# Fourth unit in the Strassen stays, joined attention groups two pairs behind, shared keys, three raw weight buffers, first loads on ScalarE's queue, halved last block

## The chip, the cores and the metric

The kernel runs on one core of a Trainium2 chip. The metric is the device time of one launch in microseconds (us); the times are medians over several runs. TensorE (PE) multiplies matrices, VectorE (DVE) and ScalarE (ACT) do the elementwise work, GpSimd (POOL) does small things, and SyncE (SP) issues the DMAs.

## The reference

Attention over 4 batches, 8 heads, 768 positions, 64 values per head, in which a query sees the 96 keys up to its own and the first 8 keys of its sequence, with a slope on the distance; behind it a gated feed-forward layer in float32:

```
keep = is_global | is_local          # first 8 keys, or 0 <= rel < 96
bias = -slopes[:, None, None] * dist[None, :, :]
scores = scores + bias[None, :, :, :]
...
a = np.exp(scores)
a = a / (np.sum(a, axis=-1, keepdims=True) + 1e-09)
x = (a @ v) as 3072 tokens x 512
out = ((x @ w_a) * (x @ w_b)) @ w_out    # w_a, w_b: 512 x 1536, w_out: 1536 x 512
```

## The kernel before

**Units and weights.** The 3072 tokens are six units of 512 tokens (`NU`, `T`). The 1536 columns of the layer are six pieces of 256, called fp 0 to 5. Weights arrive as float64 words and are turned into float32 on ACT and DVE (`to32`, the tiles `wr` for raw words and `wm` for the result). Each number is then split into a high and a low part, and a product is three matmuls (high by high, high by low, low by high).

**Passes.** `STAYS` says which pieces lie in SBUF together and which units pass over them. In the first stay (fp 0, 1, 2; units 0, 1, 2, 3) products are plain: `project_plain`, L1022, four groups of 12 matmuls 512 wide for each unit and piece. In the five later stays they are Strassen products: `project`, L1001, seven groups of 12 matmuls 256 wide, with sums on DVE (L1110) and sums of the inputs (`forms`, the tiles `xT` and `xf`). Behind either come 24 matmuls 512 wide into four accumulators (`back`, L1178). Units 0 to 3 do their remaining pieces in the stays (3, 4) and (5), units 4 and 5 do all of theirs in the later stays. Weight forms for later stays are written to DRAM (`dw`) and loaded again (`wl`).

**Attention.** A granule is one pair of heads of one unit: 24 score matmuls (`ps`, L709), the masked subtraction on DVE (L677), the exponential on ACT (L693), the sum plus 1e-9 and its reciprocal on DVE (L772, L779), the scaling on DVE or ACT (L792, L789), a transposition, and the product with the values (`pa`, L341). Unit 0 transposes on PE (L826, L827); the others transpose on DVE (L808) and go through DRAM (`mir`) into the tiles `px` and `py`. Units 1 to 3 (`LAGGED`) do the scores in two halves and the values one granule later, all as blocks of their own. Units 4 and 5 (`JOINED`) emit the scores of one granule and the values of the one before it as one block, in which matmuls on different quarters of the array stand next to each other (L709 and L322). The attention outputs of units 0 to 3 (`NEAR`) stay in the tile `X` when they are made; those of 4 and 5 go to DRAM (`dx`) and are loaded into `X` when their pass comes.

**What sets the order.** All work goes into a planner (`Schedule`): every operation has a due time, costs per engine and the buffers it takes, and the planner lists the engines' instructions in the order in which its own model would start them. The constants at the file's head (`SPANS` for attention, `CONV` for conversions, `QUADS0` and others) are due times, in passes or in nanoseconds. The engines then run in that order, each waiting only for what it needs. DMAs all go out from SP in the planned order.

**Start and end.** Before the planned part, SP loads the two counts, the position table, the slopes and the keys and queries of two granules; DVE computes the counts and a flag (L1520 to L1531) on which all engines branch. Then DVE makes the distances from the table (L604 to L608) and eight mask halves (L615). At the end `close` adds the accumulators to an earlier partial result (L1239) and writes four blocks of 128 x 512.

Of the kernel before, what the change touches and what calls it, by code (L numbers as in the profile page):

```python
# [25 lines left out]
P = 128  # L26
# [10 lines left out]
KB = KW + 64  # L37
# [8 lines left out]
KN = NH * KB  # L46
# [3 lines left out]
    ((0, 1, 2), (0, 1, 2, 3), True),  # L50
    ((3, 4), (3, 2, 1, 0), False),
    ((5,), (0, 1, 2, 3), False),
    ((5, 2), (4, 5), False),
    ((3, 4), (5, 4), False),
    ((0, 1), (4, 5), False),
)
PASSES = [(k, u) for k, stay in enumerate(STAYS) for u in stay[1]]
SPANS = {1: (0.0, 0.6), 2: (0.85, 1.6), 3: (1.6, 2.6), 4: (3, 7), 5: (6.79, 11.5)}
NEAR = (0, 1, 2, 3)
CONV = {3: (1.72, 2.88), 4: (2.5, 3.5), 5: (4.39, 7), 2: (7.27, 10), 0: (10, 12.27), 1: (11.39, 14)}  # L60
# [9 lines left out]
    "psT": (("acc3", "ga"), ("acc3",)),  # L70
}
LATER = {"psS": ("psS", "psA"), "psA": "psA", "psT": "psS"}
LAGGED = (1, 2, 3)
JOINED = (4, 5)
JOINT = 2920.0
# [6 lines left out]
WSBUFS = 2  # L82
# [3 lines left out]
FORM0 = 2410.0  # L86
START = 25980.0
LOADLEAD = 7790.0
VLAG = 13280.0
# [3 lines left out]
LAGS = {"pe": 200.0, "act": 270.0, "dve": 230.0, "pool": 290.0, "dma": 2300.0}  # L93
BIG = float(2**38)
HALF0 = 24080.0
HALF1 = 35730.0
STEPS0 = (-9.53, 6000.0, 17000.0, 25000.0)
QUADS0 = (4000.0, 3150.0, 9670.0, 13270.0, 22000.0, 25000.0)
QUADS1 = (28400.0, 31000.0, 36000.0, 35540.0, 46130.0, 44380.0)
QUADS2 = (48000.0, 51000.0, 54000.0, 51210.0, 58890.0, 63000.0)  # L100
GAP = 20220.0


def entry(u, g, i):
# [188 lines left out]
class Values:  # L293
# [91 lines left out]
    def __call__(self):  # L385
        self.main.plan.op(self.due, self.emit, self.reads, self.claim(), pe=1900)
        self.take(self.due)


class Fast:  # L390
    def __init__(self, ctx, tc, a, out, nf, ident, tiles=()):
        self.tc, self.nc = tc, tc.nc
        self.a, self.out, self.nf, self.ident = a, out, nf, ident
        self.ctx = ctx
        self.tiles = dict(tiles)
        self.plan = Schedule()
        self.count = 0
        self.granule = 0
        self.turns = 0
        self.late = None  # L400
# [51 lines left out]
    def to32(self, fp, piece, due, tag):  # L452
        nc, op = self.nc, self.plan.op
        n = f"{fp}_{piece}"
        raw = self.sbuf([P, 2 * CN], I32, "wraw", "wr" + n, 2)
# [7 lines left out]
            due - 6000.0,  # L463
# [115 lines left out]
    def load_w(self, fp, due, step):  # L579
        for j, name in enumerate(FORMS + ("O0", "O1")):  # L580
# [4 lines left out]
            self.dma(at - 5000.0, lambda st=st: st[:, :], lambda d=d: d[:, :], [d], [st], CN * 4 * P)  # L585
# [6 lines left out]
    def masks(self):  # L592
        nc, op = self.nc, self.plan.op
        ng, nl = self.nf[:, 0:1], self.nf[:, 1:2]
# [4 lines left out]
        part = lambda i: full[:, :].rearrange("p a b -> p (a b)")[:, i * n : i * n + n]  # L599
        rel, key, tmp = (lambda: part(0)), (lambda: part(1)), (lambda: part(2))  # L600

        def steps(e):
            v = nc.vector
            v.tensor_scalar(tmp(), rel(), nl, BIG, op0=ALU.is_ge, op1=ALU.mult)  # L604
            v.tensor_scalar(key(), key(), ng, BIG, op0=ALU.is_ge, op1=ALU.mult)
            v.tensor_add(rel(), rel(), tmp())
            v.tensor_scalar(key(), key(), nl, None, op0=ALU.add)
            v.tensor_tensor(rel(), rel(), key(), op=ALU.min)  # L608

        op(-2e5, steps, [], [full], port=BOTH, dve=3 * dve(n, True) + 2 * dve(n))  # L610
        for hd in range(H):
            p, h = divmod(hd, 2)
            op(
                -1e5 + hd if p < 2 else 4000.0 + hd,
                lambda e, p=p, h=h, hd=hd: nc.vector.tensor_scalar(  # L615
                    self.mask[p][:, h].rearrange("p a b -> p (a b)"),
                    rel(),
                    self.slope[:, hd : hd + 1],
                    None,
                    op0=ALU.mult,  # L620
                ),
# [3 lines left out]
                dve=dve(n, True),  # L625
# [22 lines left out]
    def granule_ops(self, u, p, due, x, d, before):  # L648
# [57 lines left out]
        def score(i, h, bank, c0, s, c, k, w):  # L706
            rows = slice(64 * h, 64 * h + 64)
            q0, k0 = i * P, QN + i * KB
# [11 lines left out]
        if u in JOINED:  # L720
# [3 lines left out]
            ahead = before  # L724
# [21 lines left out]
            before = None  # L746
        for r in () if u in JOINED else range(2):
# [10 lines left out]
            op(due, scores, [qk], ps, pe=720)  # L758
# [6 lines left out]
        if u not in DIRECT:  # L765
            tt = self.sbuf([P, 6, 2 * NH * 32], F32, "tt", "tt" + n, TTBUFS)
        for half in range(2):
            js = range(4 * half, 4 * half + 4)
            jw = slice(4 * half, 4 * half + 4)
            op(  # L770
                due,
                lambda e, jw=jw: nc.vector.tensor_scalar_add(sm[:, 2, jw], sm[:, 1, jw], 1e-9),  # L772
                [(sm, j) for j in js],
                [(sm, ("d", half))],
                dve=70,
            )
            op(
                due,
                lambda e, jw=jw: nc.vector.reciprocal(sm[:, 3, jw], sm[:, 2, jw]),  # L779
                [(sm, ("d", half))],  # L780
                [(sm, ("r", half))],
                dve=80,
            )
            flat = lambda: t[:, :].rearrange("p a b c -> p (a b) c")

            def norm(e, js=js, jw=jw):
# [3 lines left out]
                else:  # L790
                    for j in js:
                        nc.vector.tensor_scalar(  # L792
                            flat()[:, j], flat()[:, j], sm[:, 3, j : j + 1], None, op0=ALU.mult
                        )

            ts = [(t, j) for j in js]
            op(due, norm, [(sm, ("r", half))], ts, port=BOTH, dve=4 * dve(KW, True), act=4 * (act(KW) + 100))

            if u in DIRECT:
                for i in range(2 * half, 2 * half + 2):  # L800
                    self.direct(u, p, n, i, due, t, px, py)
# [11 lines left out]
            op(due, turn, ts, [(tt, half)], dve=dve(512) + dve(256))  # L813
        if u not in DIRECT:
            self.carry(n, due, tt, px, py)

        return Values(self, u, p, vt, px, py, x, d, due + VLAG)

    def direct(self, u, p, n, i, due, t, px, py):
        nc = self.nc  # L820
        self.turns += 1
        bank = self.bank(self.early_bank("psT", u, p, self.turns), f"pt{n}_{i}")

        def turn(e):
            for h in range(2):
                nc.tensor.transpose(bank[:104, h * P : h * P + P], t[:, i, h, :KX], self.ident)  # L826
                nc.tensor.transpose(  # L827
                    bank[:64, 256 + h * P : 256 + h * P + P], t[:, i, h, KX:], self.ident
                )

        self.plan.op(due, turn, [(t, 2 * i), (t, 2 * i + 1)], [bank], pe=4 * 109 + 60)
        self.copy(
            due,
            lambda: px[:104, :, 2 * i : 2 * i + 2].rearrange("p g j k -> p j g k"),
            lambda: bank[:104, :256].rearrange("p (j g k) -> p j g k", j=2, g=4),
            256,
            [bank],
            [(px, ("b", i))],
            psum=True,
        )  # L840
        for s in range(2):
            self.copy(
                due,
                lambda s=s: py[64 * s : 64 * s + 64, 2 * s : 2 * s + 2, 2 * i : 2 * i + 2].rearrange(
# [836 lines left out]
```

## Time and profile before

| What | before |
|---|---|
| median of 3 runs | 722.39 us (721.56 to 723.73) |
| time of the profiled execution | 722.86 us |
| its span from first to last instruction | 721.0 us |
| mean granted TensorE clock | 0.990 |
| ACT busy | 384.9 us (53%) |
| DMA moved | 162.43 MB, mean 225 GB/s |

The span leaves out 1.9 us of the profiled time that lie around it. Times inside the trace count from the start of the span. PE, the busiest engine, is read stretch by stretch further down. Busy time of PE is modelled: matmuls overlap, so a row's duration is longer than the distance to the next matmul, and costs of PE work are taken from distances between starts.

### The profile page before, as it was taken

Reading aid. Unit: us, or ns where it says so; the run is one execution under the profiler, and the core shown is the slowest. Engines: PE = TensorE matmul, PEld = TensorE weight load, DVE = VectorE, ACT = ScalarE, POOL = GpSimd, SP = SyncE. Lnnn points to the kernel's source line nnn. Section 1 sums busy time; section 2 is a strip of 40 time slices with the busy share of each in tenths; the row PEclk is TensorE's granted clock in tenths of the full one; section 3 lists DMA queues with packets and bytes.
Section 4 is the critical chain, followed back from the end, with each engine's and each line's share of the span. In section 5 each row is a group of like instructions: output and inputs, shape, how many; then the busy total and the mean of one; then the engine's idle time right before and its main releaser. Section 6 shows DMA issues by size and latency. Waiting matters only on the chain.

```text
span 721.0 us, 15565 instructions
## 1 busy us (share of the span) xinstructions
PE 685.9 (95%) x5808; PEld 602.3 (84%) x5808; DVE 581.6 (81%) x1552; ACT 384.9 (53%) x988; POOL 1.8 (0%) x8
## 2 busy tenths in 40 slices
PE   5598999999999999999999999999999999999995
PEld 4487877777777888888999998999898999999994
DVE  7999897878697776899899997999988558646652
ACT  5988675845565674566554546566434434424220
POOL 1000000000000000000000000000000000000000
PEclk9889999999999999999999999999999999999998
DMA  8547888998989997776786888748893423533121
GB/s 299 190 165 284 252 270 294 314 287 285 293 295 293 264 322 250 255 243 213 260 295 234 302 262 282 261 161 275 292 293 142 132 81 97 160 117 103 59 75 63
DMA packets 67910, 162.43 MB, mean 225 GB/s; under 512 B 8433, under 2 KB 21873, under 8 KB 66033
## 3 DMA queue, kind: packets, MB, share of 16 engines
q1 hardware_dynamic: 67824, 161.34, 67.7%
q8 instruction: 48, 0.79, 0.4%
q14 instruction: 38, 0.30, 0.1%
HBM read 110.45 MB, written 50.86 MB: 224 GB/s over the span
## 4 chain that ended last, share of the span: by engine, by line
PE 70%; DVE 13%; DMA 10%; ACT 4%; issue 2%; SPq 0%; ACTq 0%; DVEq 0%
PE acc L1178 22%; PE al L1001 16%; PE ga L1001 12%; PE ps L709 4%; DMA wr<-wts 3%; PE pa L341 3%; DMA qk<-qk 2%; DMA wl_A<-dw_A 1%; DVE t L677 1%; DVE tt L808 1%; DMA X<-dx 1%; DVE t L792 1%; DVE wm L495 1%; PE ps_al L322 1%; ACT wm L470 1%
## 5 line engine op out<-in xcount | busy, mean ns | idle before, releaser
L1178 PE MATMUL acc<-w_O,hh 128*128 128x512 f32 x576 | 197.0, 400 | 0.0
L1178 PEld LDWEIGHTS acc<-w_O,hh 128*128 128x128 f32 x576 | 108.3, 188 | 24.9 <-issue 1.5
L1178 PE MATMUL acc<-w_O,hl 128*128 128x512 f32 x288 | 113.7, 395 | 0.8 <-DVE hl L443 0.8
L693 ACT ACTIVATE t<-t,sm 128x168 f32<-128x168 f32 x192 | 81.1, 425 | 15.7 <-DVE sm L677 15.6
L1001 PE MATMUL al<-xf_T,w_S 128*128 128x256 f32 x576 | 76.7, 283 | 0.7 <-ACT s L433 0.7
L1001 PEld LDWEIGHTS al<-xf_T,w_S 128*128 128x128 f32 x576 | 72.4, 189 | 1.4 <-ACT s L433 0.9
L1178 PEld LDWEIGHTS acc<-w_O,hl 128*128 128x128 f32 x288 | 54.3, 188 | 10.8 <-DVE hl L443 1.4
L433 ACT CAST hh<-h 128x512 fp32r<-128x512 f32 (+1 forms) x61 | 36.0, 592 | 48.2 <-DVE h L443 23.6
L470 ACT ACTIVATE wm<-wr 128x512 f32<-128x512 f32 x54 | 36.2, 671 | 42.6 <-DMA wr<-wts 25.5
L709 PEld LDWEIGHTS ps<-qk 64*64 64x64 f32 x1056 | 32.8, 141 | 26.7 <-issue 14.0
L433 ACT COPY s<-al 128x512 f32<-128x512 f32 x44 | 25.7, 584 | 54.0 <-PE al L1001 53.8
L443 DVE TENSOR_TENSOR hl<-h,hh 128x512 fp32r<-128x512 f32 (+1 forms) x78 | 49.8, 644 | 4.9 <-ACT hh L433 4.5
L709 PE MATMUL ps<-qk 64*64 64x104 f32 (+2 forms) x1056 | 39.3, 276 | 14.5 <-DMA qk<-qk 7.1
L677 DVE CUSTOM_DVE_ANT_0 t<-ps,mask 128x168 f32<-128x168 f32 x176 | 48.6, 326 | 3.2 <-PE ps L709 3.0
L1110 DVE TENSOR_TENSOR s<-ga,s 128x512 f32<-128x512 f32 x48 | 32.8, 684 | 15.2 <-PE ga L1001 15.0
L808 DVE STREAM_TRANSPOSE tt<-t 128x512 f32<-128x512 f32 x80 | 40.9, 553 | 1.2 <-DMA mir<-tt 0.6
L1001 PE MATMUL ga<-xf_T,w_S 128*128 128x256 f32 x288 | 38.5, 283 | 1.1 <-DVE s L1110 1.0
L1001 PEld LDWEIGHTS al<-xf_B,w_A 128*128 128x128 f32 x288 | 37.5, 188 | 2.2
L505 ACT ACTIVATE wr<-wr 128x512 int32<-128x512 uint32 x54 | 36.1, 672 | 4.8 <-DVE xf_B L443 2.6
L1001 PE MATMUL ga<-xf_B,w_A 128*128 128x256 f32 x288 | 38.3, 283 | 0.3 <-DVE s L1110 0.3
L1001 PEld LDWEIGHTS ga<-xf_T,w_S 128*128 128x128 f32 x288 | 36.4, 188 | 2.6 <-DVE s L1110 2.0
L1001 PE MATMUL al<-xf_T,w_A 128*128 128x256 f32 x288 | 38.5, 283 | 0.1
(292 smaller groups left out, 1351.5 us busy)
## 6 DMA issues: line engine op xcount, KB each, us to landing
wr<-wts SPq DMA_DIRECT2D x54, 512.0 KB
qk<-qk SPq DMA_DIRECT2D x24, 720.0 KB
mir<-tt SPq DMA_DIRECT2D x20, 768.0 KB
vt<-vd SPq DMA_DIRECT2D x24, 512.0 KB
X<-dx SPq DMA_DIRECT2D x10, 1024.0 KB
part<-o SPq DMA_DIRECT2D x32, 256.0 KB
wl_S<-dw_S SPq DMA_DIRECT2D x32, 256.0 KB
px<-mir SPq DMA_DIRECT2D x60, 128.0 KB
```

The lines of the kernel that those rows point to most:

```text
L341: self.main.nc.tensor.matmul(self.banks[0][64 * h : 64 * h + 64, o : o + P], self.vt[:lanes, v0 : v0 + 64], src[:, :, 2 * i + h], start=c ...
L433: self.nc.scalar.copy(out(), src())
L443: lambda e: self.nc.vector.tensor_tensor(out(), a(), b(), op=op),
L470: lambda e: nc.scalar.activation(m(), high().bitcast(F32), AF.Abs),
L505: lambda e: nc.scalar.activation(low(), low().bitcast(U32), AF.Copy, scale=2.0**-29),
L677: lambda e: nc.vector.tensor_tensor_reduce(t[:, i, h], bank[:, c0 : c0 + KW], self.mask[pair][:, h, kind], -0.125, 3.0e38, ALU.add, ALU.mi ...
L693: lambda e: nc.scalar.activation(t[:, i, h], t[:, i, h], AF.Exp, bias=sm[:, 0, j : j + 1], scale=-1.0, accum_out=sm[:, 1, j : j + 1],),
L709: nc.tensor.matmul(bank[64 * s : 64 * s + 64, c0 + c : c0 + c + w], qk[rows, q0 + 64 * s : q0 + 64 * s + 64], qk[rows, k0 + k : k0 + k + w ...
L808: nc.vector.transpose(dst[:, :, e0 : e0 + n], src[:, :, c0 : c0 + 32 * n].rearrange("p j (e k) -> p j e k", e=n),)
L1001: self.nc.tensor.matmul(bank[:, ab * HT : ab * HT + HT], w[:, a, (2 * ab + c) * P : (2 * ab + c) * P + P], x[:, b, c], start=first, stop=F ...
L1110: lambda e: nc.vector.tensor_tensor(s[:, :], bank[:, :], s[:, :], op=ALU.add),
L1178: self.nc.tensor.matmul(acc[i][:, :], a[:, rows], w[:, b], start=first and f == 0 and k == 0, stop=False, skip_group_check=True,)
```

## The change

1. `STAYS` loses its lists of units; `TURNS` holds them. Unit 3 leaves the first stay. It passes over fp 3 and 4 behind unit 1, opens the stay (5, 2) with units 4 and 5 after it, and ends the kernel over fp 0 and 1. The number of passes stays 18.
2. Unit 3 joins `JOINED` and leaves `NEAR` and `LAGGED`. The values in a joined block are those of the granule two before (`BEHIND`), and granules wait in one list through units 3, 4 and 5.
3. The keys of neighbouring blocks are stored once: 1152 columns for a granule in place of 1440 (unit 0: 1248, in an array of its own).
4. Raw weight words get three buffers in place of two, and weight forms that are loaded again three in place of two.
5. The first keys and queries are loaded in two halves from ACT's queue. The distances are made ahead of the branch with two ACT and two DVE operations in place of five DVE operations, and mask halves may go to ACT.
6. The sum plus 1e-9 goes to POOL, once for eight columns outside unit 0. Where DVE scales, it does four columns in one operation. Unit 0's first two granules copy two transposed blocks at a time out of PSUM.
7. The last accumulator is computed, added and written in two halves.
8. All due times are new.

```diff
-    ((0, 1, 2), (0, 1, 2, 3), True),
...
+    ((0, 1, 2), True),
...
+TURNS = ((0, 1, 2), (2, 1, 3, 0), (0, 1, 2), (3, 4, 5), (5, 4), (4, 5, 3))
-NEAR = (0, 1, 2, 3)
+NEAR = (0, 1, 2)
-LAGGED = (1, 2, 3)
-JOINED = (4, 5)
+LAGGED = (1, 2)
+JOINED = (3, 4, 5)
+BEHIND = 2
-WSBUFS = 2
+WSBUFS = 3
+WRBUFS = 3
...
-        raw = self.sbuf([P, 2 * CN], I32, "wraw", "wr" + n, 2)
+        raw = self.sbuf([P, 2 * CN], I32, "wraw", "wr" + n, WRBUFS)
...
-            ahead = before
+            ahead = self.waiting.pop(0)[0] if len(self.waiting) == BEHIND else None
...
+                for _, carry in self.waiting[:1]:
+                    carry()
...
+        def sums(jw, js, k):
+            op(
+                due,
+                lambda e: nc.gpsimd.tensor_scalar_add(sm[:, 2, jw], sm[:, 1, jw], 1e-9),
...
-                    for j in js:
-                        nc.vector.tensor_scalar(
-                            flat()[:, j], flat()[:, j], sm[:, 3, j : j + 1], None, op0=ALU.mult
-                        )
+                    nc.vector.tensor_tensor(
+                        flat()[:, jw],
+                        flat()[:, jw],
+                        sm[:, 3, jw].unsqueeze(2).to_broadcast([P, 4, KW]),
+                        op=ALU.mult,
+                    )
...
+                cuts = ((0, 256), (256, 512)) if split and f == 1 and i == 3 else ((0, 512),)
...
         nc.sync.dma_start(nv, a["ns"].to_broadcast([P, 2]))
+        nc.scalar.dma_start(tiles["qk0"][:, :RUN], a["qf"][0, :, :RUN])
+        nc.sync.dma_start(table[:, :width], a["pos"][:, :width])
+        nc.scalar.dma_start(tiles["qk0"][:, RUN:], a["qf"][0, :, RUN:])
+        nc.sync.dma_start(tiles["slope"], a["pos"][:, width:])
+        nc.sync.dma_start(tiles["qk1"], a["qf"][1])
...
+def build_distances(nc, few, far, table):
+    n = 2 * KW
+    rel, key, tmp = (table[:, i * n : i * n + n] for i in range(3))
+    nc.scalar.activation(tmp, rel, AF.Relu, bias=far[:, 1:2], scale=BIG)
+    nc.scalar.activation(key, key, AF.Relu, bias=far[:, 0:1], scale=BIG)
+    nc.vector.tensor_add(rel, rel, tmp)
+    nc.vector.scalar_tensor_tensor(rel, key, few[:, 1:2], rel, op0=ALU.add, op1=ALU.min)
```

On DVE at the start, from the branch on all flags to the first masked subtraction, there stood in the kernel before:

```order
L1558 COMPARE_AND_BRANCH
L604 TENSOR_SCALAR X<-X,nf 128x336
L605 TENSOR_SCALAR X<-X,nf 128x336
L606 TENSOR_TENSOR X<-X 128x336
L607 TENSOR_SCALAR X<-X,nf 128x336
L608 TENSOR_TENSOR X<-X 128x336
L615 TENSOR_SCALAR mask_154<-X,slope 128x336 x2
L615 TENSOR_SCALAR mask_157<-X,slope 128x336 x2
L677 ISA t_0_160,sm_0_161<-ps_0_0_0_114,mask_154 128x168
```

In the changed kernel the same place of DVE's queue, with the two distance operations ahead of the branch, is:

```order
L1639 TENSOR_TENSOR X<-X 128x336
L1640 SCALAR_TENSOR_TENSOR X<-X,counts 128x336
L1621 TENSOR_LOAD flag
L1624 COMPARE_AND_BRANCH
L622 TENSOR_SCALAR mask_132<-X,slope 128x336
L622 TENSOR_SCALAR mask_139<-X,slope 128x336
L622 TENSOR_SCALAR mask_143<-X,slope 128x336
L622 TENSOR_SCALAR mask_160<-X,slope 128x336
L684 ISA t_0_162,sm_0_163<-ps_0_0_0_118,mask_132 128x168
```

Five operations on the table became two, and four mask halves (one of each pair of heads) are left; the other four stand in ACT's queue.

On PE, in the kernel before, the values of unit 3's first granule (`pa`; `px` and `py` are the transposed weights of attention, `vt` the values) stand as a block of their own between two plain groups of unit 2's pass, and the scores of unit 3's third granule follow as another block:

```order
L1022 MATMUL al_1_1(0, 1)_2742<-xp_3_2454,w_A_0_924 128x512 x3
L341 MATMUL pa_0_2767<-px_248,vt_0_2406 64x128 x2
L341 MATMUL pa_0_2767<-py_133,vt_0_2406 64x128 x2
...
L1022 MATMUL ga_1_1(0, 1)_2794<-xp_0_2333,w_A_0_852 128x512 x3
...
L709 MATMUL ps_2_0_0_2814<-qk_78 64x168
L709 MATMUL ps_2_0_1_2816<-qk_78 64x168
```

In the changed kernel the values of unit 3 stand in shared blocks. This one, in the second stay, ends the scores of unit 4's first granule (`ps_0`), goes on with the values of unit 3's third granule (`vt_2`, the one two before), and is followed by accumulation:

```order
L716 MATMUL ps_0_al<-qk_59 64x64
L716 MATMUL ps_0_ga<-qk_59 64x64
L336 MATMUL ps_0_al<-py_135,vt_2_2967 64x64 x2
L336 MATMUL ps_0_ga<-py_135,vt_2_2967 64x64 x2
...
L336 MATMUL ps_0_al<-px_246,vt_2_2967 64x64 x2
L336 MATMUL ps_0_ga<-px_246,vt_2_2967 64x64 x2
...
L1226 MATMUL acc_3_2772<-w_O_192359_2936,hh_3_1_3262 128x512
```

Unit 3's values moved out of blocks of their own into blocks shared with scores, and from the first stay's end into the second stay; there are ten shared blocks in place of seven.

More of the change, by code (lines that the diff above doesn't have):

```diff
@@ L36 @@
 KW = KX + 64
-KB = KW + 64
+KB = NG + P
 T = 512
@@ L399, in __init__ @@
         self.turns = 0
-        self.late = None
+        self.waiting = []
     def open(self):
@@ L766, in granule_ops @@
             tt = self.sbuf([P, 6, 2 * NH * 32], F32, "tt", "tt" + n, TTBUFS)
+        whole = u not in DIRECT
+        def sums(jw, js, k):
+            op(
+                due,
+                lambda e: nc.gpsimd.tensor_scalar_add(sm[:, 2, jw], sm[:, 1, jw], 1e-9),
+                [(sm, j) for j in js],
+                [(sm, ("d", k))],
+                pool=170,
+            )
+            op(
+                due,
+                lambda e: nc.vector.reciprocal(sm[:, 3, jw], sm[:, 2, jw]),
+                [(sm, ("d", k))],
+                [(sm, ("r", k))],
+                dve=100,
+            )
+        if whole:
+            sums(slice(0, 2 * NH), range(2 * NH), 0)
         for half in range(2):
@@ L769, in granule_ops @@
             jw = slice(4 * half, 4 * half + 4)
[L770 to L775, printed above, removed]
-            )
[L777 to L783, printed above, removed]
+            if not whole:
+                sums(jw, js, half)
             flat = lambda: t[:, :].rearrange("p a b c -> p (a b) c")
@@ L820, in direct @@
+        return then
+    def direct(self, u, p, n, blocks, due, t, px, py):
         nc = self.nc
         self.turns += 1
-        bank = self.bank(self.early_bank("psT", u, p, self.turns), f"pt{n}_{i}")
+        i0, m = blocks[0], 2 * len(blocks)
+        js = slice(2 * i0, 2 * i0 + m)
+        bx = self.bank(self.early_bank("psT", u, p, self.turns), f"pt{n}_{i0}")
+        by, c0 = (bx, 2 * P) if m == 2 else (self.bank("ga", f"pu{n}_{i0}"), 0)
         def turn(e):
[L825 to L829, printed above, removed]
@@ L831, in direct @@
-        self.plan.op(due, turn, [(t, 2 * i), (t, 2 * i + 1)], [bank], pe=4 * 109 + 60)
+            for k in range(m):
+                i, h = i0 + k // 2, k % 2
+                o = k * P
+                nc.tensor.transpose(bx[:104, o : o + P], t[:, i, h, :KX], self.ident)
+                nc.tensor.transpose(by[:64, c0 + o : c0 + o + P], t[:, i, h, KX:], self.ident)
+        self.plan.op(
+            due,
+            turn,
+            [(t, j) for j in range(js.start, js.stop)],
+            [bx] if m == 2 else [bx, by],
+            pe=m * 2 * 109 + 60,
+        )
@@ L832, in direct @@
         self.copy(
             due,
[L834 to L838, printed above, removed]
+            lambda: px[:104, :, js].rearrange("p g j k -> p j g k"),
+            lambda: bx[:104, : m * P].rearrange("p (j g k) -> p j g k", g=4, k=32),
+            m * P,
+            [bx],
+            [(px, ("b", i)) for i in blocks],
@@ L892, in attention @@
             self.xsaved[u] = d
-        late, self.late = self.late, None
+        late = None
         for p in range(NPAIR):
             then = self.granule_ops(u, p, dues[p], x, d, late)
-            if u in LAGGED or u in JOINED:
+            if u in LAGGED:
                 late = then
-            else:
+            elif u not in JOINED:
                 then()
-        if late and u in JOINED and u + 1 in JOINED:
-            self.late = late
-        elif late:
+        if late:
             late()
+        if u == JOINED[-1]:
+            for k, (then, carry) in enumerate(self.waiting):
+                if k:
+                    carry()
+                then()
         return x
@@ L1162, in project, with back @@
         return parts
-    def back(self, fp, due, parts, acc, first):
+    def back(self, fp, due, parts, acc, first, split):
         st = 3 * pe(512)
@@ L1280, in run @@
             t = times[i]
-            fps, _, plain = STAYS[stay]
+            fps, plain = STAYS[stay]
             if i and PASSES[i - 1][1] != u:
@@ L1287, in run @@
                     xf[u] = self.load_x(u, t - 7000.0)
-            elif i and STAYS[PASSES[i - 1][0]][2] and not plain:
+            elif i and STAYS[PASSES[i - 1][0]][1] and not plain:
                 xf[u] = self.forms(u, t - 7000.0, x)
@@ L1316, in prev @@
                 def prev(d, fp=fp, parts=parts, acc=acc, first=fresh and k == 0, over=over, u=u, i=i):
-                    self.back(fp, d, parts, acc, first)
+                    self.back(fp, d, parts, acc, first, over and i + 1 == len(PASSES))
                     d = d[-1] if isinstance(d, list) else d
```

283 lines of the change are left out of this document (155 added, 128 removed).

## The prediction

> **What bounds the kernel now.** I read the busy shares first, then busy time by stretches, then who PE waits for, and then single places in the timeline and the chain of waits. On the page:
>
> ```profile
> PE 685.9 (95%) x5808; PEld 602.3 (84%) x5808; DVE 581.6 (81%) x1552; ACT 384.9 (53%) x988; POOL 1.8 (0%) x8
> ```
>
> PE is the bound as a mean. The stretches show where it is not (columns: busy time of PE, weight loads, DVE, ACT and POOL with their instructions, granted clock, DMA share, GB/s):
>
> ```profile
> core 0: us, PE busy (x) PEld busy (x) DVE busy (x) ACT busy (x) POOL busy (x), PEclk, DMA share, GB/s
> 0.00:6.00 6.00, 0.00 (x0) 0.00 (x0) 1.33 (x10) 0.36 (x1) 0.92 (x7) 1.00 0.55 159
> 6.00:36.00 30.00, 20.21 (x269) 16.63 (x270) 29.33 (x124) 26.10 (x91) 0.90 (x2) 0.91 0.74 261
> 36.00:112.00 76.00, 69.58 (x720) 61.34 (x719) 70.38 (x248) 57.08 (x173) 0.00 (x0) 0.97 0.77 249
> 112.00:307.00 195.00, 192.40 (x1501) 152.65 (x1501) 150.31 (x445) 113.93 (x311) 0.00 (x0) 1.00 0.87 285
> 307.00:560.00 253.00, 250.66 (x2289) 230.50 (x2288) 236.81 (x563) 136.17 (x325) 0.00 (x0) 1.00 0.74 250
> 560.00:713.00 153.00, 153.00 (x1037) 141.18 (x1036) 92.71 (x168) 51.29 (x91) 0.00 (x0) 1.00 0.32 98
> 713.00:721.00 8.00, 0.02 (x1) 0.00 (x0) 0.74 (x2) 0.00 (x0) 0.00 (x0) 0.74 0.31 114
> ```
>
> From 112 to 713 us PE is idle 4.9 us in all, so there a removed matmul is worth its full time. From 6 to 36 DVE is busy 29.33 of 30 us: unit 0's attention and the first conversions run at DVE's pace. From 36 to 112, the first pass, PE and DVE are both over 90% busy, and PE is idle 6.4 us. The last 8 us are the write of the result.
>
> **Part 1: matmuls.** A plain group and a Strassen group in the chain of waits (start, length):
>
> ```profile
> 139.58 2.80 PE al_0(0, 1)_1899 L1022 x12
> ...
> 378.26 1.44 PE al L1001 x12
> ```
>
> One piece of a unit takes 4 plain groups, 4 x 2.80 = 11.20 us, or 7 Strassen groups, 7 x 1.44 = 10.08. Unit 3 changes over for three pieces: 3 x 1.12 = **-3.4 us**. The accumulation behind them stays at 24 matmuls each.
>
> A separate block of scores, a separate block of values and a joined block, from one start to the next (columns: start, length, what):
>
> ```profile
> 96.45 1.58 PE L1022 MATMUL al_0(0,)_1342<-xp,w_A 128*128 128x256 f32 x12
> 97.97 0.82 PE L709 MATMUL ps<-qk 64*64 64x168 f32 x24
> 98.72 0.50 PE L1178 MATMUL acc<-w_O,hh 128*128 128x512 f32 x1
> 99.05 0.39 PE L1178 MATMUL acc<-w_O,hl 128*128 128x512 f32 x1
> ```
>
> ```profile
> 78.67 1.60 PE L1022 MATMUL ga_1(0,)_1105<-xp,w_A 128*128 128x256 f32 x12
> ...
> 82.11 0.51 PE L1178 MATMUL acc<-w_O,hh 128*128 128x512 f32 x1
> 82.45 0.39 PE L1178 MATMUL acc<-w_O,hl 128*128 128x512 f32 x1
> ```
>
> ```profile
> 440.40 0.39 PE L1178 MATMUL acc<-w_O,hh 128*128 128x512 f32 x1
> 440.72 1.11 PE L709 MATMUL ps<-qk 64*64 64x168 f32 x36
> ...
> 443.60 0.50 PE L1178 MATMUL acc<-w_O,hh 128*128 128x512 f32 x1
> 443.94 0.39 PE L1178 MATMUL acc<-w_O,hl 128*128 128x512 f32 x1
> ```
>
> Twelve matmuls of 256 hand over after 1.44 us, one of 512 after 0.23, and the first matmul behind a block takes about 0.1 longer. So half a granule's scores cost 98.72 - 97.89 + 0.10 = 0.93, the values 82.11 - 80.11 + 0.11 = 2.11, and a joined block 443.60 - 440.63 + 0.11 = 3.08. Separate is 2 x 0.93 + 2.11 = 3.97, 0.89 more. Joined blocks go from 7 to 10: 3 x 0.89 = **-2.7 us**. Part 1 is -6.0 us, with bounds -5 and -6.5; it holds in full only while PE doesn't wait.
>
> Does DVE bear it? Strassen and the inputs' forms add, counted from the order, 20 operations of 512 and 12 of 256 columns (20 x 0.68 + 12 x 0.42 = 18.7 us), less 10 plain ones (6.8):
>
> ```profile
> L1110 DVE TENSOR_TENSOR s<-ga,s 128x512 f32<-128x512 f32 x48 | 32.8, 684 | 15.2 <-PE ga L1001 15.0
> L443 DVE TENSOR_TENSOR h<-s 128x256 f32<-128x256 f32 x72 | 29.7, 419 | 0.8
> L792 DVE TENSOR_SCALAR t<-t,sm 128x168 f32<-128x168 f32 x112 | 26.7, 301 | 0.1
> L779 DVE RECIPROCAL sm<-sm 128x4 f32<-128x4 f32 x48 | 8.2, 170 | 0.4
> L772 DVE TENSOR_SCALAR sm<-sm 128x4 f32<-128x4 f32 x48 | 7.5, 157 | 5.0 <-ACT t L693 4.9
> ```
>
> All of L772 goes (-7.5), 20 of 48 reciprocals (-3.4), and 112 scalings become 27 of 672 columns. That operation is in no row; from the 512-column row it lies between 0.68 and 0.68 x 672/512 = 0.90, and I take 0.85 (near proportion): 27 x 0.85 = 23 for 26.7. DVE ends up about 3 us lower. Between 307 and 560 it is 94% busy today and PE loses 2.3 us, so I put the middle at no change, with bounds -3 and +3.
>
> **Part 2: the start.** DVE from the branch to the first masked subtraction:
>
> ```profile
> 5.76 0.73 DVE L604 TENSOR_SCALAR X<-X,nf 128x336 f32<-128x336 f32 x1 [0.76 <-DVE flag L1531]
> 6.42 0.73 DVE L605 TENSOR_SCALAR X<-X,nf 128x336 f32<-128x336 f32 x1
> 7.07 0.49 DVE L606 TENSOR_TENSOR X<-X 128x336 f32<-128x336 f32 x1
> ...
> 8.44 1.31 DVE L615 TENSOR_SCALAR mask<-X,slope 128x336 f32<-128x336 f32 x4
> 9.66 0.32 DVE L677 CUSTOM_DVE_ANT_0 t<-ps,mask 128x168 f32<-128x168 f32 x1
> ```
>
> The distances take 8.44 - 5.76 = 2.7 us; two operations like L606 take about 1.0, so -1.7. Four of eight mask halves go to ACT, which is idle until the first exponential: 4 x 0.33 = -1.3. In unit 0, eight L772 (0.07 each to the next start) and eight scalings (about 0.1 each) give -1.4. That is 4.4 us of DVE's work in a stretch where DVE never rests. The first products start earlier by as much, and I take **-4.5 us** for the whole start. Bounds: 0, if the new order fills the place with conversions that the first pass doesn't wait for; -9, if most of DVE's rests up to 112 (5.6 + 0.7) go too. The keys (the first matmul waits until 7.1) aren't counted: DVE doesn't use the scores before 9.66.
>
> **Part 3: raw weights.** In the first pass the chain of waits runs over four long landings of raw words, the first and the last of which are:
>
> ```profile
> 78.67 5.70 DMA wr<-wts
> ...
> 119.03 4.33 DMA wr<-wts
> ```
>
> With two buffers a load is issued only when the piece two before is converted; a third gives it one conversion's time more. These 4 x 5 = 20 us are on the chain, but PE has other work meanwhile: it is idle only 6.4 us there. I take **-1.5 us**, bounds 0 and -6.
>
> **Part 4: the end.** The chain's last pieces:
>
> ```profile
> 701.82 11.22 PE acc L1178 x48
> ...
> 713.06 0.69 DVE X L1239
> ```
>
> The last addition halves from 0.69 to the 0.42 of a 256-column row (-0.3), and 7.2 us follow it, in which the last write shrinks from 256 to 128 KB; at 300 GB/s, an estimate from the 285 above, that is -0.4. I take **-0.5 us**, bounds -0.2 and -1.
>
> **Costed at nothing.** The shared keys save 3.3 MB of 162 in a queue that PE hardly waits for; without that cover they would be worth 12 us of transfer. Unit 3's way through DRAM is new: values, store, load into `X`, forms. Unit 5 shows it today:
>
> ```profile
> 530.47 1.94 PE pa L341 x32
> 533.04 3.47 DMA dx<-vt
> 536.88 7.63 DMA X<-dx
> ```
>
> From 530.5 to the load's end at 544.5 are 14 us, and the forms follow. By the order about 23 us of PE work lie between unit 3's last values and its first product (unit 5: 20 before, 23 now), so it is covered; if not, 2 or 3 us.
>
> **The sum.** 722.86 - 6.0 - 4.5 - 1.5 - 0.5 = 710.4 against the profiled execution, which lies 0.5 above the median of the runs: 709.9, given as **710 us**.
>
> **Rivals.** *The start's gain is lost.* POOL gets eight small operations into unit 0's softmax, on the way from ACT's sums to DVE's reciprocal. If each waits for the DVE operation that runs (up to 0.7 us by the rows above) and DVE then has nothing else ready, 8 x 0.7 = 5.6 us come back, as much as part 2 brings: 710 + 5.6 = 715.6. For it: DVE is busy 98% there, so something always runs. Against it: for the same reason DVE has other work while it waits. Chance 0.18. [...]
>
> *The start gains more.* PE's idle time in the first pass and in the middle goes as well: -9 in part 2, -3 in the middle: 710 - 4.5 - 3 = 702.5. Chance 0.15.
>
> *Slower: the weights for the first Strassen stay come late.* Its first matmul today (durations, then first and last start):
>
> ```profile
> L1001 PE MATMUL al<-xf_B,w_A x288: 274/282/361, 307.6 to 692.9; 128*128 128x256 f32 x144
> ```
>
> The first stay loses unit 3's 3 x (11.2 + 24 x 0.23) = 50 us of plain work and about 9 of its attention, which covered the loads of fp 3 and 4; with 6 from parts 2 and 3 the Strassen stay begins near 242 in place of 307.6. By the order SP issues 61.2 MB up to the last load for fp 3, 80.5 before: 253 GB/s are wanted in place of 262. The rows give a mean of 271 for 0 to 307 us, and 244 for the first 36. It is as slow as before when the queue moves 61.2 MB / (242 + 12.5 us) = 240 GB/s; at 235 PE stands still some 18 us: 728. Chance 0.05 for this, and 0.07 for a milder form between 716 and 724.
>
> That unit 3 stays plain or that the blocks aren't joined is no rival: the order shows both.
>
> **How the numbers follow.** Forecast (706 to 714.5): 0.55. The range takes the bounds: down to 703 (start and middle together), up to 718 (part 2 lost, with some of the middle); beyond lie the late weights and part of the larger gain. About 0.3%, 2.2 us, is what a measurement can tell from no change. Faster: 0.55 + 0.18 + 0.15 and a little of the mild form, 0.90; same 0.04; slower 0.06.
>
> **What would show it.** Part 1: 252 more Strassen matmuls and 144 fewer plain ones of 512, joined blocks at 3.1 us. Part 2: the first masked subtraction near 7.5 to 8.5, the first product near 31 in place of 35.7. Part 3: no landing of `wr` over 4 us on the chain of the first pass. Part 4: under 7.5 us from the last matmul to the end, 8.0 today. The forecast is wrong if PE waits over 5 us in sum for DVE, ACT or loads between the first pass and the last, or if the first pass ends no earlier.

## The result, and the profile after

| | before | changed |
|---|---|---|
| median of the runs shown (us) | 721.97 (720.08 to 723.73, 4 runs) | 713.72 (710.59 to 716.40, 4 runs) |
| ratio, 95% interval | | 0.9861 [0.982, 0.9901] |
| beside the experiments (us) | 721.64 (11 runs) | 714.69 (712.74 to 717.16, 6 runs), 0.9899 [0.9871, 0.9926] |
| profiled execution, its span (us) | 722.86, 721.0 | 710.59, 708.7 |
| PE busy, span less PE busy (us) | 685.9, 35.1 | 677.4, 31.3 |

The change is worth 7 to 8 us. The forecast was 710, the range 703 to 718. The busy shares on the page after:

```profile
PE 677.4 (96%) x6015; PEld 603.4 (85%) x6015; DVE 576.7 (81%) x1411; ACT 396.0 (56%) x1003; POOL 13.2 (2%) x36
```

The stretches of the changed kernel, with the columns of the prediction's table (the last two are cut at the last matmul, which now comes at 703):

```profile
core 0: us, PE busy (x) PEld busy (x) DVE busy (x) ACT busy (x) POOL busy (x), PEclk, DMA share, GB/s
0.00:6.00 6.00, 0.00 (x0) 0.00 (x0) 0.67 (x7) 0.00 (x0) 0.69 (x6) 1.00 0.53 143
6.00:36.00 30.00, 20.43 (x256) 17.10 (x260) 24.71 (x94) 26.32 (x80) 3.72 (x8) 0.89 0.69 248
36.00:112.00 76.00, 70.52 (x754) 61.64 (x745) 73.09 (x224) 64.39 (x191) 2.29 (x6) 1.00 0.79 261
112.00:307.00 195.00, 192.34 (x1745) 161.51 (x1744) 170.12 (x447) 122.47 (x335) 3.67 (x10) 1.00 0.88 294
307.00:560.00 253.00, 251.07 (x2303) 230.78 (x2303) 219.04 (x485) 137.85 (x322) 2.83 (x6) 1.00 0.72 241
560.00:703.00 143.00, 143.00 (x975) 132.40 (x973) 88.28 (x157) 44.95 (x78) 0.00 (x0) 1.00 0.28 90
703.00:709.00 6.00, 0.06 (x1) 0.00 (x0) 0.83 (x3) 0.00 (x0) 0.00 (x0) 0.84 0.45 154
```

Read the second row first. From 6 to 36 us DVE does 24.71 us of work where it did 29.33: the 4.6 us that the prediction wanted to take from DVE are gone. But PE does no more there than before (20.43, 20.21), and ACT is as full as it was (26.32, 26.10). DVE's work turned into idle time of DVE. The timeline of the start shows where it stands:

```profile
5.26 0.17 DVE L1585 CAST counts<-nv 128x2 f32<-128x2 int32 x1 [5.26 <-DMA nv<-ns]
...
7.21 1.28 ACT L1637 ACT_TABLE_LOAD   x1 [7.21 <-DMA X<-pos]
...
8.51 0.57 ACT L1637 ACTIVATE X<-X,counts 128x336 f32<-128x336 f32 x1
8.99 0.56 ACT L1638 ACTIVATE X<-X,counts 128x336 f32<-128x336 f32 x1
9.11 0.51 DVE L1639 TENSOR_TENSOR X<-X 128x336 f32<-128x336 f32 x1 [2.59 <-ACT X L1637]
...
10.57 1.31 DVE L622 TENSOR_SCALAR mask<-X,slope 128x336 f32<-128x336 f32 x4 [0.26 <-DVE X L1640]
11.80 0.33 DVE L684 CUSTOM_DVE_ANT_0 t<-ps,mask 128x168 f32<-128x168 f32 x1
```

The counts land at 5.26 (3.81 before), ACT loads its table only once the positions have landed at 7.2, DVE waits 2.59 us for ACT, and the first masked subtraction comes at 11.80, 2.1 us later than before. The first product follows at 38.52, 2.9 later than before's 35.67.

So the 8 us can't come from the start. They are PE's: seven profiles of kernels with the change's stays and its order on PE (the changed kernel twice, and `e1_queue`, `e2_table`, `e3_both`, `e10_samesums`, `e12_late3` below) have 677.4 to 681.3 us of PE busy, 678.9 in the mean, 7.0 less than before, and 31.0 to 35.3 us in which PE is idle, 33.3 in the mean against 35.1 before. PE's idle time hardly moved. Up to the second pass, which begins with the first plain matmuls 512 wide, PE has 1088 matmuls in either kernel, so the change's matmuls all lie behind it. From there to the last matmul the granted clock is 1.00, and PE is busy, in the kernel before and in the changed one:

```profile
125.31:713.02 587.71, 584.47 (x4724) 514.82 (x4720) 470.72 (x1152) 294.29 (x712) 0.00 (x0) 1.00 0.67 222
```

```profile
122.17:703.05 580.88, 577.76 (x4932) 517.52 (x4927) 468.49 (x1069) 299.72 (x723) 6.50 (x16) 1.00 0.66 220
```

The seven profiles have 577.8 to 579.2 us there, 578.4 in the mean: 6.1 us less than before, and no part of that is clock.

### The profile page after: what moved, and what is told of

Read it like the earlier page. It is cut to its first block, busy times and chain, and to the rows that moved or that the text cites. A ratio compares the mean times of both kernels' runs of the same rounds, so it can differ in the third digit from the quotient of the medians.

```text
span 708.7 us, 15928 instructions
## 1 busy us (share of the span) xinstructions
PE 677.4 (96%) x6015; PEld 603.4 (85%) x6015; DVE 576.7 (81%) x1411; ACT 396.0 (56%) x1003; POOL 13.2 (2%) x36
## 4 chain that ended last, share of the span: by engine, by line
PE 55%; DVE 19%; DMA 14%; ACT 7%; issue 3%; SPq 1%; POOL 0%; DVEq 0%; ACTq 0%; POOLq 0%
PE acc L1226 18%; PE al L1046 15%; PE ga L1046 12%; DMA wr<-wts 7%; ACT t L700 3%; PE ps L716 2%; DVE tt L835 2%; DVE wm L526 2%; PE pa L355 2%; DVE wm L509 2%; DVE t L684 2%; DMA part<-o 1%; DVE wm L491 1%; DMA py<-mir 1%; DVE hl L457 1%
## 5 line engine op out<-in xcount | busy, mean ns | idle before, releaser
L1046 PE MATMUL al<-xf_T,w_S 128*128 128x256 f32 x648 | 86.6, 283 | 0.2 <-ACT s L447 0.2
L1046 PEld LDWEIGHTS al<-xf_T,w_S 128*128 128x128 f32 x648 | 81.3, 189 | 1.2 <-ACT s L447 0.6
L716 PE MATMUL ps<-qk 64*64 64x168 f32 (+2 forms) x1008 | 36.9, 282 | 12.4 <-DVE flag L1596 7.3
L1046 PEld LDWEIGHTS al<-xf_B,w_A 128*128 128x128 f32 x324 | 42.2, 189 | 3.8 <-DVE sm L684 1.5
L1046 PE MATMUL ga<-xf_T,w_S 128*128 128x256 f32 x324 | 43.2, 283 | 1.3 <-DVE s L1155 1.3
L1046 PE MATMUL al<-xf_B,w_A 128*128 128x256 f32 x324 | 43.2, 283 | 0.9 <-DVE sm L684 0.9
L1046 PE MATMUL ga<-xf_B,w_S 128*128 128x256 f32 x324 | 43.2, 283 | 0.5 <-ACT s L447 0.5
L1046 PE MATMUL ga<-xf_B,w_A 128*128 128x256 f32 x324 | 43.1, 283 | 0.0
L1046 PE MATMUL al<-xf_T,w_A 128*128 128x256 f32 x324 | 43.0, 282 | 0.0
L1046 PEld LDWEIGHTS ga<-xf_T,w_S 128*128 128x128 f32 x324 | 40.9, 189 | 2.0 <-DVE s L1155 1.5
```

Of the source, the lines that this page charges most:

```text
L716: nc.tensor.matmul(bank[64 * s : 64 * s + 64, c0 + c : c0 + c + w], qk[rows, q0 + 64 * s : q0 + 64 * s + 64], qk[rows, k0 + k : k0 + k + w ...
L1046: self.nc.tensor.matmul(bank[:, ab * HT : ab * HT + HT], w[:, a, (2 * ab + c) * P : (2 * ab + c) * P + P], x[:, b, c], start=first, stop=F ...
```

## The experiments

Where an experiment changes what the planner sees, the planner orders the whole program anew; this is said each time, and in `e4_sums` it mattered more than the edit. The kernels ran in three groups, each on one chip with the kernel before beside them, so across groups the ratios to before are compared.

**The start, three ways.** The changed kernel again, beside them:

> The changed kernel once more, beside the experiments on the start, so that each is compared with it on the same chip. From its four runs so far (710.6 to 716.4) a median near 713.5 is expected, and a spread of some 5 us, where the kernel before spreads by 3.6.

Measured: 714.69, spread 4.4 us.

`e1_queue` puts the first keys back on SP's queue:

```diff
-        nc.scalar.dma_start(tiles["qk0"][:, :RUN], a["qf"][0, :, :RUN])
         nc.sync.dma_start(table[:, :width], a["pos"][:, :width])
-        nc.scalar.dma_start(tiles["qk0"][:, RUN:], a["qf"][0, :, RUN:])
         nc.sync.dma_start(tiles["slope"], a["pos"][:, width:])
+        nc.sync.dma_start(tiles["qk0"][:, :RUN], a["qf"][0, :, :RUN])
+        nc.sync.dma_start(tiles["qk0"][:, RUN:], a["qf"][0, :, RUN:])
         nc.sync.dma_start(tiles["qk1"], a["qf"][1])
```

> Unit 0's keys go back to SP's queue, behind the counts, the positions and the slopes; nothing else moves. Theory A (the two key loads on ScalarE's queue delay the small load of the counts, which landed at 5.26 in place of 3.81): the counts start near 3.8 again and the positions land before 7.2, the first masked subtraction comes 1.0 to 1.5 us earlier than 11.80, and the whole is 1 to 1.5 us shorter. Theory B (the delay at the start is absorbed by the attention of unit 0, whose first product waits for other things): the first masked subtraction moves, the first product (38.5) and the whole stay within 0.7 us. Theory C (the late landing has nothing to do with the second queue): nothing moves.

`e2_table` loads ACT's table while the positions are on their way (the block keeps the written order):

```diff
-        nf, flag, few, far = build_counts(nc, cp, nv)
-        build_distances(nc, few, far, table)
+        warm = cp.tile([P, 1], F32, name="warm")
+        with tc.manual_schedule():
+            nc.scalar.activation(warm, ident[:, 0:1], AF.Relu)
+            nf, flag, few, far = build_counts(nc, cp, nv)
+            build_distances(nc, few, far, table)
```

> A one-column Relu of a ready tile stands ahead of the counts, so that ACT's table load (1.28 us at 7.21, behind the positions' landing) is done before they land. Theory A (the table load lies on the way to the first masked subtraction): that comes at 10.5 in place of 11.80, the whole is up to 1.3 us shorter. Theory B (absorbed): the first product and the whole stay within 0.7 us.

`e3_both` has both edits:

> Both edits together. Theory A: first masked subtraction at 8.7 to 9.2, first product near 35.5 in place of 38.5, the whole 2 to 3 us shorter, near 710.5 where the changed kernel stands at 713.5. Theory B (absorbed): the whole is as before this edit, within 0.7 us.

| | counts start | first masked subtraction | first product | whole, ratio |
|---|---|---|---|---|
| before | 3.81 | 9.66 | 35.67 | 721.64 |
| changed (profile of the result) | 5.26 | 11.80 | 38.52 | 714.69, 0.9899 [0.9871, 0.9926] |
| e1_queue | 3.74 | 9.68 | 36.70 | 715.40, 0.9922 [0.9893, 0.9951] |
| e2_table | 5.38 | 10.43 | 37.16 | 714.07, 0.9886 [0.9857, 0.9915] |
| e3_both | 3.73 | 8.39 | 36.78 | 712.97, 0.9867 [0.9835, 0.9898] |

Both causes of the late start are shown: the second queue delays the counts by 1.5 us, the table load costs 1.3. Together they bring the first masked subtraction to 8.39, inside the prediction's 7.5 to 8.5. Yet of the 3.4 us only 1.7 reach the first product, no more than `e1_queue` brings alone (1.8), and it comes at 36.78 where 35.5 was expected. Up to the first masked subtraction theory A holds. For the whole, `e1_queue` lies 0.7 us above the changed kernel, `e2_table` 0.6 and `e3_both` 1.7 below it, all with overlapping intervals: the runs can't tell 0 from the 1 to 3 us that were expected. With the start mended, the chain of waits of `e3_both` shows what took over (start, length, what):

```profile
6.19 2.62 PE ps L716 x32
8.81 0.02 issue
8.83 7.52 DMA qk<-qf
16.35 0.14 issue
16.48 1.40 PE ps L716 x16
```

The keys of the third pair are issued at 8.83 and land 7.5 us later. In that stretch (5 to 18 us) the queue of `e3_both`, and behind it that of the kernel before, has (packets, MB, share of the 16 engines):

```profile
q1 hardware_dynamic: 1203, 4.41, 92.6%
```

```profile
q1 hardware_dynamic: 1103, 4.79, 97.9%
```

So in `e3_both` the chain hangs on a transfer there, though PE has other work meanwhile and stands idle for these keys only 1.4 us, up to 16.48. (The 6.2 us that the next expectation names are PE's wait for the first keys, at the program's start.) In the kernel before the engines were as full, but its chain of waits runs through ACT from 15.4 on (shown further down); in the changed kernel they are busy 79.5% of this stretch. `e12_late3` is `e3_both` with one transfer moved: the third raw piece, which the third buffer lets in early, is issued behind the first values:

```diff
         order, end = self.plan.order()
+        raw = [o for o in order if any(b.tag == "wraw" for b in o.bufs) and "dma" in o.costs]
+        keys = [o for o in order if any(b.tag == "vt" for b in o.bufs) and "dma" in o.costs]
+        order.remove(raw[2])
+        order.insert(order.index(keys[0]) + 1, raw[2])
```

> Both edits of the start (keys on SP's queue, the table loaded early), and the load of the third raw piece is issued behind the first values of unit 0 in place of ahead of the fourth pair's keys; no other order changes. With the two edits alone the third pair's keys were issued at 8.83 and landed at 16.35, PE waiting 6.2 us for them, while the DMA engines were 93% busy from 5 to 18 us. Theory A (the start is bound by transfers, and the third raw piece takes the place of the keys): the keys land near 13, PE's wait falls to about 3 us, the first product comes at 34 to 35.5 in place of 36.8, the whole 1 to 2 us shorter than with the two edits alone (713.0). Theory B (what follows, ScalarE's queue of work above all, sets the first product): it stays within 0.7 us of 36.8, and the whole at 713.

Measured: 716.25, ratio 0.9924 [0.99, 0.9947]. PE's wait for the third pair's keys, 1.4 us in `e3_both`, is gone; but the first product comes at 38.48, later than in `e3_both`. Its chain says why:

```profile
12.97 7.63 DMA wr<-wts
20.60 0.02 issue
20.63 0.68 ACT wm L484
```

The raw piece now lands at 20.60, its conversion begins then, and the weights wait in place of the keys. Neither theory had this: in this stretch, which transfers nearly fill (92.6% in `e3_both`, 92.2% here), the other order of transfers exchanged one wait for another.

**The additions on POOL.** `e4_sums` gives them back to DVE and tells the planner so, `e10_samesums` gives them to DVE at the places where POOL had them, all else in the changed kernel's order:

```diff
-                lambda e: nc.gpsimd.tensor_scalar_add(sm[:, 2, jw], sm[:, 1, jw], 1e-9),
+                lambda e: nc.vector.tensor_scalar_add(sm[:, 2, jw], sm[:, 1, jw], 1e-9),
...
-                pool=170,
+                dve=70,
```

(the last two lines in `e4_sums` alone)

> The changed kernel with its 28 additions to the sums of the softmax back on DVE (the planner is told so, and sets its order by it). In the trace of the changed kernel such an addition takes 0.22 us on POOL where DVE does nothing with two inputs, and up to 0.74 where it stands beside one. Theory A (POOL's stretched additions hold up unit 0 and with it the whole): 2 to 5 us shorter than the changed kernel (714), near 710 to 712. Theory B (DVE has other work meanwhile; eight more DVE operations of 0.07 to 0.16 us in unit 0 cost about what the wait costs): within 1.5 us of it.

> The changed kernel with its 28 additions run by DVE, each at the place where the planner has POOL's; the order of everything else on every engine is that of the changed kernel. With DVE's additions and a new order the kernel lost some 7 us (721.8). Theory A (the loss came from the new order, and where the additions run is worth little): 713 to 716, as the changed kernel. Theory B (the loss came from the additions on DVE): 720 or more. Theory C (POOL's stretched additions were a loss): 710 to 712.

Measured: 721.65, 0.9981 [0.9958, 1.0003] for `e4_sums` (11 of its 12 runs; the other took 729.9), and 714.17, 0.9894 [0.9865, 0.9923] for `e10_samesums`. So where the additions run is worth nothing that can be measured, and the 6 us that `e4_sums` lies above `e10_samesums` (by the ratios) are those of a new order for which no due time was set. The longer additions themselves are in the trace. In the changed kernel's timeline, an addition on POOL while DVE stands idle, and one beside a DVE operation on two tensors:

```profile
14.18 0.23 POOL L780 TENSOR_SCALAR sm<-sm 128x4 f32<-128x4 f32 x1 [5.85 <-ACT t L700]
...
15.56 0.85 DVE L807 TENSOR_TENSOR t<-t,sm 128x672 f32<-128x672 f32 x1
...
15.75 0.74 POOL L780 TENSOR_SCALAR sm<-sm 128x4 f32<-128x4 f32 x1 [1.34 <-ACT t L700]
```

The second ends at 16.49, just behind DVE's at 16.41: the addition took 0.74 us beside that operation and 0.23 alone. All 28 on POOL take between 0.22 and 0.745 us, 0.39 in the median; in `e10_samesums`, on DVE, they take 0.154 to 0.173.

**Raw buffers.** Two in place of three in the changed kernel (`e5_wr2`), and three in place of two in the kernel before (`b1_wr3`), each with a new order:

```diff
-WRBUFS = 3
+WRBUFS = 2
```

```diff
-        raw = self.sbuf([P, 2 * CN], I32, "wraw", "wr" + n, 2)
+        raw = self.sbuf([P, 2 * CN], I32, "wraw", "wr" + n, 3)
```

> The changed kernel with two buffers of raw words in place of three; the planner orders around it. Theory A (the third buffer is worth its term of the prediction): 1.5 us longer, 715.5 or so. Theory B (PE has other work while raw words land): within 1 us. Theory C (the first pass lives by it): 4 us or more longer, and PE's idle time between 36 and 112 us grows by as much.

> The kernel before with a third buffer of raw words, and nothing else of the change; the planner orders around it, so the third piece is loaded ahead of the third pair's keys. Theory A (the third buffer is worth 1.5 us, as the prediction has it): 720. Theory B (it is worth what the changed kernel loses without it): 715 or less. Theory C (it is worth nothing by itself, and a new order without due times set for it costs): 722 or more.

Measured: 730.7 for `e5_wr2`, 1.0115 [1.0077, 1.0154] (four of its six runs; the two others took 738.9 and 740.1), that is 2.2% or 16 us above the changed kernel; and 725.14, 1.0032 [1.0011, 1.0054], 2.3 us above the kernel before. By the times these are theories C of both expectations. But the profile of `e5_wr2`, of the run of 738.9, has 11.1 us of PE's idle time from 36 to 112 us where the changed kernel has 5.5, so the first pass's idle time holds only a part of the loss. Each program's due times were set for the buffers it has, which may be why the same buffer is worth much in one and less than nothing in the other; that isn't shown, since both runs have a new order. The buffer's own worth at the changed kernel's order stays open: no run holds that order with two buffers.

**Unit 3's stays, and two pairs behind.** `e7_unit3plain` puts unit 3 back, `e8_turnalone` moves it in the kernel before (its `STAYS` get the units of `TURNS`, and it takes the changed kernel's due times for attention and conversions, `SPANS` and `CONV`; joined groups stay one pair behind), and `e9_behind1` is the changed kernel with joined groups one pair behind. All three have new orders; `e7_unit3plain` has the `SPANS` and `CONV` of before:

```diff
-TURNS = ((0, 1, 2), (2, 1, 3, 0), (0, 1, 2), (3, 4, 5), (5, 4), (4, 5, 3))
+TURNS = ((0, 1, 2, 3), (3, 2, 1, 0), (0, 1, 2, 3), (4, 5), (5, 4), (4, 5))
...
-LAGGED = (1, 2)
-JOINED = (3, 4, 5)
+LAGGED = (1, 2, 3)
+JOINED = (4, 5)
```

```diff
-BEHIND = 2
+BEHIND = 1
```

> The changed kernel with unit 3 back in the plain stay and its blocks separate (the tables of turns, spans, conversions, near, lagged and joined units are those of before; everything else is the change's). Theory A (the gain is PE's work): 6.0 us longer than the changed kernel's 714, near 720, and 144 plain matmuls more, 252 Strassen matmuls fewer. Theory B (the gain comes from the start, the loads and the end): within 2 us of the changed kernel. The due times weren't set for these tables, which can add some us.

> The kernel before with unit 3 moved to the Strassen stays and its blocks joined, and nothing else of the change (its start, its two raw buffers, its whole last block, its sums and scalings stay; the joined groups stay one pair behind). Theory A (the gain is PE's work): 6.0 us shorter than before's 721.6, near 715.6, that is nearly all that the whole change brings. Theory B: within 2 us of before. Rival C (the weights of the first Strassen stay come late without the third buffer): longer than before, with PE waiting for loads near 240 us.

> The changed kernel with joined groups one pair behind in place of two; the planner orders around it. Theory A (the second pair covers the way of a softmax through DRAM): PE waits for px and py from mir some 10 us or more in sum between 400 and 560 us, in the changed kernel under 1, and the whole is 5 to 20 us longer. Theory B (one pair is cover enough): within 2 us of the changed kernel.

Measured: `e7_unit3plain` 729.62, 1.0119 [1.0077, 1.0161], 16 us above the changed kernel. Its page, to be held against 677.4 to 681.3:

```profile
PE 688.1 (95%) x5779; PEld 604.2 (83%) x5779; DVE 566.2 (78%) x1383; ACT 392.9 (54%) x996; POOL 12.7 (2%) x36
```

Some 7 to 11 us are PE's work, and 726.0 - 688.1 = 37.9 us of idle time are 2.6 more than the most of the seven. Theory A is right in kind. Its 6.0 should have been 7.0: with groups two pairs behind only six joined blocks are left (384 matmuls of L336, 64 in a block), not seven, so that by the prediction's prices 3.4 + 4 x 0.89 come back. The other 9 of the 16 us came with the new order and aren't taken apart further. All the rest of the change, without unit 3's move and at these due times, is thus 1.2% slower than the kernel before.

`e8_turnalone` took 767.96, 1.0626 [1.0595, 1.0656], where theory A had 715.6, and `e9_behind1` 780.64, 1.0825 [1.0781, 1.087]. Both have the cheaper stays, and PE stands still. Whom PE waits for in `e8_turnalone` and in `e9_behind1` (sum, times, longest):

```profile
PE pa L341 <- DMA px<-mir: 24.0, 4, 16.6
PE al L1001 <- ACT xf_B L433: 10.4, 2, 8.1
PE ps_al L322 <- DMA py<-mir: 9.9, 1, 9.9
```

```profile
PE ps_al L336 <- DMA py<-mir: 19.5, 2, 10.9
PE pa L355 <- DMA px<-mir: 15.6, 1, 15.6
PE al L1046 <- ACT xf_B L447: 12.9, 3, 8.3
```

In the changed kernel the same list, between 400 and 560 us, has none of the three. A wait for loaded weights, as in rival C, is not among the waits of `e8_turnalone`; PE waits for the softmax. The chain of waits of `e9_behind1` shows the longest of these waits, the 15.6 us for `px`:

```profile
548.25 0.33 DVE t L684
...
549.28 3.35 ACT t L700 x16
...
554.23 1.97 DVE tt L835 x4
556.22 3.25 DMA mir<-tt
...
560.83 3.07 DMA px<-mir
563.91 0.14 issue
```

With one pair of lag and nothing else to do, PE waits for all of it: 8.0 us of softmax on DVE and ACT, and 7.7 us of the way through DRAM (`mir`). The granted clock falls too: on the page of `e9_behind1` it is 5 tenths in the three slices from 522.8 to 580.9 us. Of the loss of 66 us, 50 are idle time of PE (83.7 us, in the mean of the seven profiles 33.3) and 12 are in its busy time (690.8, in their mean 678.9). In `e8_turnalone` the clock is 5 tenths in the two slices from 537.2 to 575.6, and its PE busy time, 686.7, is no lower than before's; so no run shows the worth of the cheaper stays by themselves.

In the expectation for `e9_behind1` theory A was right in kind, and its 5 to 20 us too small. Both runs have due times of units 3 to 5 that were set for groups two pairs late, and the kernel before, one pair behind with due times of its own, waits for `mir` 0.6 us at most. How much of the loss is the lag and how much these due times stays open.

## Why the prediction was right, and where not

- **Part 1, matmuls, -6.0: right, and nearly the whole result.** 252 more Strassen matmuls (2016 to 2268) and 144 fewer plain ones (720 to 576) are in the trace as forecast. A joined block of the changed kernel takes 433.52 - 430.54 + 0.11 = 3.09 us by its rows, where 3.08 was taken:

```profile
430.31 0.39 PE L1226 MATMUL acc<-w_O,hh 128*128 128x512 f32 x1
430.63 1.11 PE L716 MATMUL ps<-qk 64*64 64x168 f32 x36
...
433.52 0.50 PE L1226 MATMUL acc<-w_O,hh 128*128 128x512 f32 x1
```

  PE busy fell by 7.0 in the mean, 6.1 of them behind the second pass, where the clock is 1.00; the other 0.9 lie ahead of it, where the granted clock differs from profile to profile (from 36 to 112 us it is 0.97 in the kernel before, 1.00 and 0.96 in the changed kernel's two profiles). It rises by 7 to 11 when unit 3 goes back. PE is idle 4.6 us from 112 us to its last matmul, before 4.9: the middle was no change, as forecast. The first Strassen stay begins at 239.1, where 242 was forecast.
- **What Part 1 stands on was missed.** "Costed at nothing" weighed unit 3's values and not the softmax's way through `mir`. In the changed kernel PE doesn't wait for it; with one pair of lag in place of two, at the same due times, 66 us are lost.
- **Part 2, the start, -4.5: wrong; it lost 2.9 at the first product.** The sizes on DVE were right (4.4 forecast, 4.6 measured; the 672-column scaling took 0.85 as estimated). The step that failed is "the first products start earlier by as much", which rests on "run at DVE's pace". The same stage row had ACT at 26.10 of 30 us, the transfers were at 97.9% from 5 to 18, and from 15.4 to 30.3 the chain of waits of the kernel before runs almost wholly through ACT, for instance:

```profile
15.44 0.37 ACT px L433
...
19.69 3.35 ACT t L693 x16
...
29.61 0.63 ACT w_A L433
```

  DVE's share alone was read. Two small losses came on top, 1.5 us for the counts behind the second queue and 1.3 for the table load. In the profile of the result the delay is made up by the second pass, which begins at 122.2, before at 125.3; in the changed kernel's second profile it begins at 126.6, behind two stretches in which the clock reads 0.50 (62 to 64 and 110 to 112 us). Whether the first pass ends earlier, which the prediction named as a sign, differs from run to run.
- **Part 3, the third buffer, -1.5: not borne out.** Landings over 4 us stayed on the first pass's chain:

```profile
89.34 5.93 DMA wr<-wts
97.91 6.49 DMA wr<-wts
104.94 4.51 DMA wr<-wts
```

  Why they are as long as before isn't shown. With a new order around it, the buffer cost the kernel before 2.3 us.
- **Part 4, the end, -0.5: not shown.** From the last matmul to the end are 708.7 - 703.1 = 5.6 us where 8.0 were, in the second profile 715.0 - 707.7 = 7.3. Between them lies one issue of a write on SP (0.40 us in the one, 1.93 in the other), whose cause stays open. `b1_wr3` and `e8_turnalone` end as the kernel before does, with a whole last block, and take 722.2 - 715.9 = 6.3 and 767.5 - 760.2 = 7.3 us. So the same end differs by more than the 0.5 us from profile to profile, and the under 7.5 us that the prediction named as a sign come without the halving too.
- **The sum.** -6.0 was the result; of the other -6.5 about 1.8 came (PE's mean idle time, 33.3 for 35.1). That is why it came out some 4 us above the forecast. The range held because its upper end allowed for a lost start.
- **The rivals.** "The start's gain is lost" has the right time (715.6) by another mechanism: POOL's additions take longer beside DVE's operations, as it supposed, but unit 0's eight take 3.6 us in sum, at 0.23 each 1.8, so 1.8 us more and not 5.6; and by `e10_samesums` they cost nothing that can be measured. "The start gains more" fell with Part 2. "Weights late" did not come; the cliff that the experiments found is the softmax and its way through DRAM.

## What to carry to other kernels

Where three resources are full in one stage, taking work from the fullest engine may buy no more than the distance to the next (here DVE had 29.33 of 30 us and ACT 26.10, and with 4.6 us off DVE the first product came 2.9 later); read all the columns of that stage's row, the DMA share in short stretches too, before a gain is booked. Under a planner with hand-set due times, undoing one edit measures the edit and a new order together, and the order was worth 6 us where the edit was worth nothing: repeat the edit with the order held fixed. Look for what covers the longest round trip before counting cheaper work behind it.

## What the runs showed of the hardware

In the changed kernel's second profile a wait of 2.9 us on PE is followed by a stretch at a lower granted clock; the first profile has neither there. The second profile, two microseconds to a row (columns as above, the clock third from the end):

```profile
106.00:108.00 2.00, 0.50 (x5) 0.30 (x3) 2.00 (x6) 0.00 (x0) 0.00 (x0) 1.00 0.24 57
108.00:110.00 2.00, 0.60 (x3) 0.60 (x4) 1.06 (x3) 1.22 (x3) 0.00 (x0) 0.76 0.37 92
110.00:112.00 2.00, 2.00 (x11) 2.00 (x11) 0.71 (x2) 0.00 (x0) 0.00 (x0) 0.50 0.93 235
112.00:114.00 2.00, 2.00 (x22) 1.58 (x23) 0.69 (x1) 1.42 (x3) 0.00 (x0) 0.89 1.00 416
```

PE waits 2.9 us for ACT, up to 109.40, and the clock reads 0.76, 0.50 and 0.89 in the rows from 108 us on. By these rows that is 2 x (0.24 + 0.50 + 0.11) = 1.7 us of clock. In the first profile of the same kernel this wait is 0.6 us long, and the clock is 1.00 in all four rows. The group of 12 matmuls that waited, in the second profile and in the first:

```profile
109.40 2.93 PE L1067 MATMUL al_1(1,)_1481<-xp,w_A 128*128 128x256 f32 x12 [2.90 <-ACT s_0(1,)_1477 L447]
```

```profile
105.40 1.71 PE L1067 MATMUL al_1(1,)_1481<-xp,w_A 128*128 128x256 f32 x12 [0.64 <-ACT s_0(1,)_1477 L447]
```

The second profile has another such stretch: the clock is 0.81 from 60 to 62 us and 0.50 from 62 to 64; of the 2 us from 58 and the 2 us from 60, PE was busy 0.81 and 1.19. In the first profile PE was busy 0.81 and 1.44 there, and the clock is 1.00 from 58 to 64 us. So the same kernel has such a stretch in one profile and not in the other; what sets it off isn't shown. Over the changed kernel's ten runs the mean clock goes from 0.987 to 0.995; the four at 0.994 and above took 710.6 to 713.8 us, the six others 713.5 to 717.2. That is more than any of the start's edits brought, but it is a correlation over ten runs, and the twelve runs of `e12_late3` don't have it: 719.07 us at 0.999, 713.78 at 0.989.
